# Attention ramp in another order, tokens laid out chunk by chunk, the row of maxima turned by TensorE

## Chip, cores and metric

One core of one Trainium2 chip. The metric is the device time of one execution in microseconds (us), the median of three runs. TensorE (PE) multiplies, its weight loads (PEld) overlap the products; VectorE (DVE), ScalarE (ACT) and GpSimd (POOL) do the rest; SyncE (SP) issues most of the DMAs, GpSimd and ScalarE a few through queues of their own.

## What is computed

An attention over hash buckets, then two feed-forward layers. The change touches the attention alone.

```python
B, H, S, D = 2, 8, 768, 64          # 16 heads of 768 tokens, 64 wide; 6 hash bits
q_bits = q @ proj > 0 ; k_bits = k @ proj > 0
mask = bucket(q_bits)[:, None] == bucket(k_bits)[None, :]
scores = where(mask, q @ k.T / 8, -1e9)
attn = exp(scores - scores.max(-1)) ; attn /= attn.sum(-1) + 1e-9
x = attn @ v                        # then a top-1 mixture of 8 experts and a gated layer
```

## The kernel before, in words

The whole kernel is one stream of instructions per engine, written out by hand: what a Python function emits first stands first in its engine's queue, and an engine that waits holds everything behind it.

The attention stage takes the 16 heads one after the other. A head has 768 keys and 768 queries, cut into `NC` = 6 chunks of `P` = 128 keys; a step `k` is one chunk of one head (96 steps, 6 per head). For each head four tiles stand ready in one of four `sets`: `X` and `K2` hold the scaled high halves of queries and keys and, in rows 64 to 75, the signs of the hash bits; `X` has the row of the queries' maxima in row 76, and `K2` has -1 there, so that one product subtracts the maximum. `K1` and `Y` hold high and low halves crosswise. The steps of a head:

- `prep` (L396) and, for the first three heads, `prep0` (L379): ScalarE makes the high half `hi`, VectorE (GpSimd for heads 0 and 1) the low half `lo`, DMAs of SP bring them to their rows; `put_bits` (L409) brings the signs, two DMAs of SP. `bits` (L419) makes the signs of four heads at a time: TensorE passes (L428), then two passes of VectorE (L417).
- `mx` (L448) takes one chunk of 128 queries against all keys, two products (L454), and VectorE reduces each to its maximum (L457). The chunk's queries are every sixth column, `c::NC`, because query `6p + c` is partition `p` of chunk `c`. After the sixth chunk VectorE makes `top` (L460), 128 x 6, and a DMA (L461) writes it as one row of `X`.
- `scores` (L463): per chunk of keys two halves of 384 queries, two products each (L471, L472), and ScalarE's exponential (L473), which also puts the queries into the order chunk by chunk.
- `high` and `low` (L478, L485) split the exponentials in two halves of 16 bits; `pv` (L489) multiplies them with the values, for two steps at once at odd `k`; `evac` (L521) moves a head's result out.

The values come in groups of four heads (`load_v`, `vmax`, `vscale`, `vsplit`, `vgate`): their largest value fixes a scale (`vscale`, small products L610 and L619 and a chain of small VectorE passes), then `vsplit` (L711) makes their halves, ScalarE the high one (L717), VectorE the low one (L719).

The order: lines 729 to 789 write the ramp up to the first scores, then a loop over `k` (L871) emits per step: what is due before it, ScalarE's high half of step `k-1`, the scores of `k`, the low half of step `k-2` (GpSimd), the maxima of the chunk eight steps ahead (`AHEAD` for the first eight steps, from `Q['ac']`), the value products at odd `k`, what is due after it. `at`, `spread` and `stages` give due times in steps; `load_r` loads a head's queries and keys (384 KB, six buffers). `heat` issues products of zeros that nobody reads. The maxima of head `h` are complete in step `6h - 3`, and its first scores are step `6h`.

## Time and profile before

| | us |
|---|---|
| median of three runs (661.36 to 662.96) | 661.85 |
| the profiled execution | 664.08 |
| its span, first to last instruction | 662.3 |
| first exponential of the attention starts | 19.55 |
| last stage of the attention is over, about | 230 |

TensorE is busy for 95% of the span, VectorE 71%, ScalarE 66%, GpSimd 35%. The chain of work that ended last can be followed back to 230.74 us, where the program branches; the attention stage before it has to be read from tables of stretches and from the engines in order of time. TensorE's products are pipelined: a product's own duration is longer than its distance to the next, so distances between starts are what counts.

### The profile page before, as it was taken

What the parts mean: (1) busy time and instruction counts of PE and PEld (TensorE: products, weight loads), DVE (VectorE), ACT (ScalarE), POOL (GpSimd) and SP (SyncE); (2) the same over time, 40 slices, a digit from 0 to 9 for tenths busy, and PEclk for the clock granted to TensorE, in tenths of its full rate; (3) what the DMA queues carried; (4) which work ended last, traced back from release to release, by engine and by line L of the source; (5) the groups of instructions that cost most, each with busy time, mean ns of one, the idle gap of its engine ahead of it and who ended that gap; (6) DMA issues with size and microseconds to landing.
All of it is one profiled execution on the core that took longest, in us unless ns stands there. A gap on an engine that the chain in (4) does not pass through costs nothing.

```text
span 662.3 us, 14355 instructions
## 1 busy us (share of the span) xinstructions
PE 630.1 (95%) x5497; PEld 469.5 (71%) x5497; DVE 472.1 (71%) x1042; ACT 435.1 (66%) x880; POOL 232.2 (35%) x217
## 2 busy tenths in 40 slices
PE   6999999999999799999999999999999999999892
PEld 2678889889888669999999995555555555555440
DVE  6788988888879888888888888888888342222410
ACT  8658868878878746777776755455545585555820
POOL 6457879879896052111566300000000030000021
PEclk9999999999999989999999999999999999999997
DMA  5645864774465158777677643443441020000011
GB/s 195 175 125 136 243 168 125 237 184 126 103 176 187 57 174 309 242 249 236 214 248 253 212 138 107 141 154 131 127 147 46 0 80 17 0 1 1 0 50 52
DMA packets 37843, 92.18 MB, mean 139 GB/s; under 512 B 8986, under 2 KB 14362, under 8 KB 37762
## 3 DMA queue, kind: packets, MB, share of 16 engines
q1 hardware_dynamic: 34674, 83.75, 41.9%
q0 software_dynamic: 2400, 7.36, 3.2%
q8 instruction: 46, 0.75, 0.5%
q14 instruction: 35, 0.29, 0.1%
q10 hardware_dynamic: 688, 0.03, 0.1%
HBM read 67.14 MB, written 6.29 MB: 111 GB/s over the span
## 4 chain that ended last, share of the span: by engine, by line
PE 55%; ACT 3%; DMA 3%; DVE 2%; issue 1%; POOL 0%; POOLq 0%
PE psg L1332 17%; PE pso L1359 15%; PE psy L1110 11%; PE psh L1083 10%; DMA out_dram<-os,inv 3%; ACT junk L1286 2%; PE psa L1060 1%; ACT gh L1342 1%; DVE rl L1335 1%; DVE wl L164 1%; PE heat L1162 0%; ACT rl L1334 0%; ACT wh L158 0%; ACT hh L1086 0%; PE heatt L335 0%
## 5 line engine op out<-in xcount | busy, mean ns | idle before, releaser
L487 POOL TENSOR_TENSOR plo<-pf,phi 128x768 f16<-128x768 f32 x86 | 144.9, 1706 | 32.8 <-ACT phi L481 16.7
L457 DVE TENSOR_REDUCE mx<-psm 128x1 f32<-128x384 f32 x192 | 96.8, 550 | 20.6 <-PE psm L454 19.9
L473 ACT ACTIVATE pf<-pst 128x384 f32<-128x384 f32 x192 | 83.4, 486 | 40.3 <-PE pst L472 35.8
L1374 POOL DMA_INDIRECT out_dram<-os,inv x12 | 12.1, 1012 | 272.6 <-DVE os L1366 244.3
L164 DVE SCALAR_TENSOR_TENSOR wl<-raw,wh 128x1024 f16<-128x1024 f32 (+1 forms) x68 | 82.5, 1216 | 6.2 <-ACT wh L158 5.4
L1332 PE MATMUL psg<-yTh,ch 128*128 128x512 f16 (+1 forms) x256 | 83.4, 326 | 3.2 <-DVE rl L1335 3.2
L1332 PE MATMUL psg<-yTl,ch 128*128 128x512 f16 (+1 forms) x256 | 83.4, 326 | 0.0
L1332 PE MATMUL psg<-yTh,cl 128*128 128x512 f16 (+1 forms) x256 | 83.4, 326 | 0.0
L1335 DVE SCALAR_TENSOR_TENSOR rl<-rl,psg 128x512 f32<-128x512 f32 x64 | 35.0, 551 | 64.4 <-ACT rl L1334 64.0
L471 PE MATMUL pst<-Y,K 128*128 128x384 f32 x192 | 75.7, 394 | 2.3 <-ACT pf L473 2.3
L1332 PEld LDWEIGHTS <-ch 128*128 128x128 f16 x512 | 50.1, 98 | 35.9
L481 ACT ACTIVATE phi<-pf 128x768 f16<-128x768 f32 x85 | 71.7, 844 | 1.9
L1359 PE MATMUL pso<-ch,gh 128*128 128x512 f16 x192 | 72.8, 379 | 0.0
L1359 PE MATMUL pso<-ch,gl 128*128 128x512 f16 x192 | 72.8, 379 | 0.0
L1359 PE MATMUL pso<-cl,gh 128*128 128x512 f16 x192 | 72.8, 379 | 0.0
L158 ACT ACTIVATE wh<-raw 128x1024 f16<-128x1024 f32 (+1 forms) x68 | 67.4, 998 | 0.8 <-DVE offs L959 0.8
L1359 PEld LDWEIGHTS <-gh 128*128 128x128 f16 x384 | 37.6, 98 | 42.3
L454 PE MATMUL psm<-K,X 76*128 76x384 f32 x192 | 64.3, 419 | 2.8 <-DVE mx L457 1.1
L472 PE MATMUL pst<-X,K 77*128 77x384 f32 x192 | 66.3, 346 | 0.5 <-DMA X<-top 0.5
L1110 PE MATMUL psy<-hh,wl 128*128 128x224 f16 x256 | 66.3, 259 | 0.2 <-DVE wl L164 0.2
L1110 PE MATMUL psy<-hh,wh 128*128 128x224 f16 x256 | 66.3, 259 | 0.0
L1110 PE MATMUL psy<-hl,wh 128*128 128x224 f16 x256 | 66.3, 259 | 0.0
(243 smaller groups left out, 1485.6 us busy)
## 6 DMA issues: line engine op xcount, KB each, us to landing
raw<-in_w_dram SPq DMA_DIRECT2D x64, 512.0 KB
rc<-in_win_dram SPq DMA_DIRECT2D x16, 512.0 KB
rc<-in_wout_dram SPq DMA_DIRECT2D x16, 512.0 KB
r<-in_qk_dram SPq DMA_DIRECT2D x16, 384.0 KB
K<-hi SPq DMA_DIRECT2D x26, 192.0 KB
vr<-in_v_dram SPq DMA_DIRECT2D x4, 768.0 KB
vt<-in_vt_dram SPq DMA_DIRECT2D x8, 384.0 KB
K<-lo SPq DMA_DIRECT2D x16, 192.0 KB
```

Of the source, the lines that this page charges most:

```text
L158: act.activation(wh[e, i][:, c : c + n], r, AF.Copy, scale=(S1, S2)[i // 2])
L164: dve.scalar_tensor_tensor(out=wl[e, i][:, c : c + n], in0=r, scalar=(S1, S2)[i // 2], in1=wh[e, i][:, c : c + n], op0=ALU.mult, op1=ALU.s ...
L457: dve.tensor_reduce(out=mm[:, c, n : n + 1], in_=ps[:, :HS], axis=AX.X, op=ALU.max)
L471: pe.matmul(ps[:, :HS], st["K1"][:, kc], st["Y"][:, qc], start=True, stop=False)
L472: pe.matmul(ps[:, :HS], st["K2"][0:77, kc], st["X"][0:77, qc], start=False, stop=True)
L473: act.activation(pf.rearrange("k (c n p) -> k c n p", c=NC, n=2)[:, :, n], ps[:, :HS].rearrange("k (p c) -> k c p", c=NC), AF.Exp, scale=0 ...
L481: act.activation(phi_t[k], pf_t[k], AF.Copy)
L487: eng.tensor_tensor(out=plo_t[k], in0=pf_t.pop(k), in1=phi_t[k], op=ALU.subtract)
L1083: pe.matmul(ps, l[:, c], r[:, k], start=n == 0, stop=n == 3 * KD - 1)
L1110: pe.matmul(ps, l, r, start=n == 0, stop=n == 3 * KF - 1)
L1332: pe.matmul(ps, l, x, start=n == 0, stop=n == 3 * KD - 1)
L1359: pe.matmul(po[blk][s], l, r, start=first and n == 0, stop=last and n == 2)
```

## The change

- The host lays out queries, keys and values so that the tokens of a chunk (`6p + c` for all `p`) lie together. `mx` then reads a contiguous block of `X`, and the exponential writes straight through.
- The row of maxima: `top` is turned by a transpose on TensorE into 6 x 128, VectorE copies it to a tile `rowm`, and a DMA of six pieces writes the row. `turn` is called in the step after the one that ends the head's maxima, ahead of the next `mx`.
- The ramp: the first head's maxima have a filler product behind each chunk, its row is turned after half of the sign passes, the first scores come ahead of the products of the scale, `put_bits` for heads 1 and 2 uses SP for `X` and GpSimd's queue for `K2`, the rest of `pre[1]`, `pre[2]` and the load of head 4 come later.
- Values of heads 0 and 1: ScalarE also scales `r` in place, GpSimd subtracts for the low half.
- Due times: `pre[2]` ends at 5.5; head 3 is prepared at 7 and 8.25 in place of 2.25 and 5.25; loads of heads 8 to 15 come at -11.5, -10.75, -10 and -4 steps from the group's first step in place of -2 to -1.25; one chunk of maxima moves from step 2 to step 1 and one from step 3 to step 2.

```diff
-'ac': (0, 0, 2, 4, 6, 7, 8, 10)
+'ac': (0, 1, 3, 4, 6, 7, 8, 10)
...
-        top = pa.tile([P, NH, NC], F32R, tag="top", name="top")
+        top = pa.tile([P, NH, NC], F32, tag="top", name="top")
+        rowm = [pa.tile([NC, P], F32R, tag=f"rm{i}", name=f"rm{i}") for i in range(2)]
+        turns = []
...
         def put_bits(h):
             st = sets[h % 4]
+            q = pool if h < 3 else sp
...
-            sp.dma_start(out=f32(st["K2"])[D : D + 12], in_=f32(b)[o + 12 : o + 24])
+            q.dma_start(out=f32(st["K2"])[D : D + 12], in_=f32(b)[o + 12 : o + 24])
...
                 for n in range(2):
                     for i in range(4):
                         dot(n, i)
-                yield
+                    yield
...
-                    ps[:, :HS], st["X"][0:76, c::NC], st["K2"][0:76, n * HS : (n + 1) * HS], start=True, stop=True
+                    ps[:, :HS], st["X"][0:76, c * P : (c + 1) * P], st["K2"][0:76, n * HS : (n + 1) * HS], start=True, stop=True
...
-                sp.dma_start(out=f32(st["X"])[76:77, :].rearrange("o (p c) -> o p c", c=NC), in_=f32(top)[:, h])
+                turns.append(h)
+
+        def turn(h):
+            ps = ps_m.tile([P, 512], F32, tag="m", name=f"pstop{h}")
+            pe.transpose(ps[0:NC, 0:P], top[:, h], ident)
+            dve.tensor_copy(rowm[h % 2], ps[0:NC, 0:P])
+            row = f32(sets[h % 4]["X"])[76:77, :].rearrange("o (c p) -> o c p", c=NC)
+            sp.dma_start(out=row, in_=f32(rowm[h % 2]))
...
-                act.activation(
-                    pf.rearrange("k (c n p) -> k c n p", c=NC, n=2)[:, :, n],
-                    ps[:, :HS].rearrange("k (p c) -> k c p", c=NC), AF.Exp, scale=0.125 / SC / SC,
-                )
+                act.activation(pf[:, qc], ps[:, :HS], AF.Exp, scale=0.125 / SC / SC)
...
             act.activation(t[:, :, o : o + D], r, AF.Copy, scale=s)
+            if h in (0, 1):
+                act.activation(r, r, AF.Copy, scale=s)
             yield
+            lo = t[:, :, VA + o : VA + o + D]
+            if h in (0, 1):
+                pool.tensor_tensor(out=lo, in0=r, in1=t[:, :, o : o + D], op=ALU.subtract)
+            else:
+                dve.scalar_tensor_tensor(
+                    out=lo, in0=r, scalar=s, in1=t[:, :, o : o + D], op0=ALU.mult, op1=ALU.subtract
+                )
...
         for n in range(NC):
             mx(n)
-        run(pre[1])
-        load_r(4)
+            heat(ps_x, "x", 1)
+        next(b0)
+        turn(turns.pop())
         next(b0)
         for i in range(4):
             vmax(0, i)
         vs = vscale(0)
         next(vs)
+        scores(0)
+        next(b0)
+        next(b0)
+        put_bits(1)
         next(vs)
-        next(b0)
-        heat(ps_t, "t", 2)
+        heat(ps_v, "v", 1)
         next(vs)
         next(vs)
-        next(b0)
-        put_bits(1)
-        scores(0)
-        run(b0)
+        put_bits(2)
         run(vs)
-        next(pre[2])
-        put_bits(2)
-        run(pre[2])
+        run(pre[1])
+        load_r(4)
...
+        at(5.5, run, pre[2])
...
-            at(max(0, 24 * (h // 4 - 1) - 2) + h % 4 / 4, load_r, h)
+            at(24 * (h // 4 - 1) + (-11.5, -10.75, -10, -4)[h % 4], load_r, h)
...
-                spread(2.25, prep(h), 3)
+                stages(prep(h), (7, 8.25))
...
+            while turns:
+                turn(turns.pop())
             for n in AHEAD[k] if k < len(AHEAD) else (k + LEAD,):
```

## Rows read from the trace of the kernel before

**Rows 1.** Table of stretches: ends, length, busy us and instructions of each engine.
```profile
core 0: us, PE busy (x) PEld busy (x) DVE busy (x) ACT busy (x) POOL busy (x), PEclk, DMA share, GB/s
128.05:177.65 49.60, 49.31 (x613) 43.69 (x612) 43.14 (x106) 41.44 (x78) 42.03 (x35) 1.00 0.57 148
19.56:52.06 32.50, 30.09 (x268) 22.93 (x268) 25.80 (x58) 21.97 (x41) 18.79 (x11) 1.00 0.44 130
```

**Rows 2.** Groups by line, 70 to 180 us: weight loads, busy us and mean ns.
```profile
L454 PEld LDWEIGHTS psm<-K,X 76*128 76x128 f32 x107 | 29.0, 315 | 0.1
L472 PEld LDWEIGHTS pst<-X,K 77*128 77x128 f32 x106 | 20.2, 190 | 0.0
```

**Rows 3.** TensorE in order of time, two steps: start us, us, instruction.
```profile
107.29 0.42 PE L471 MATMUL pst<-Y,K 128*128 128x384 f32 x1
...
107.91 0.34 PE L472 MATMUL pst<-X,K 77*128 77x384 f32 x1
108.09 0.62 PE L454 MATMUL psm<-K,X 76*128 76x384 f32 x2
108.55 0.27 PE L610 MATMUL psn<-ident,am 128*1 128x128 f32 x1
108.58 0.42 PE L471 MATMUL pst<-Y,K 128*128 128x384 f32 x1
...
111.07 0.42 PE L471 MATMUL pst<-Y,K 128*128 128x384 f32 x1
```

**Rows 4.** ScalarE in order of time, exponentials of the same steps.
```profile
107.99 0.87 ACT L473 ACTIVATE pf<-pst 128x384 f32<-128x384 f32 x2 [0.39 <-PE pst L472]
...
109.65 0.85 ACT L473 ACTIVATE pf<-pst 128x384 f32<-128x384 f32 x2
...
111.77 0.87 ACT L473 ACTIVATE pf<-pst 128x384 f32<-128x384 f32 x2 [0.40 <-PE pst L472]
```

**Rows 5.** Groups by line and shape, ScalarE reading PSUM, whole span.
```profile
L473 ACT ACTIVATE pf<-pst 128x384 f32<-128x384 f32 x192 | 83.4, 486 | 40.3 <-PE pst L472 35.8 <-POOL plo L487 4.3
...
L1086 ACT ACTIVATE hh<-psh 128x224 f16<-128x224 f32 x64 | 22.6, 353 | 17.5 <-PE psh L1083 16.4 <-issue 0.6 <-PE psc L936 0.5
...
L1063 ACT ACTIVATE xh<-psa 128x448 f16<-128x448 f32 x16 | 8.7, 545 | 7.9 <-PE psa L1060 6.7
```

**Rows 6.** In order of time, the row of head 1: SP's issue, TensorE's use.
```profile
33.29 0.51 SPq L461 DMA_DIRECT2D X<-top  x1
...
35.39 0.41 PE L472 MATMUL pst<-X,K 77*128 77x384 f32 x1 [0.46 <-DMA X<-top]
```

**Rows 7.** In order of time, head 4: VectorE ahead of step 22's maxima, TensorE in step 24.
```profile
73.50 0.61 DVE L517 TENSOR_TENSOR xp<-psv,rd 128x432 f32<-128x432 f32 x1
...
76.99 0.34 PE L472 MATMUL pst<-X,K 77*128 77x384 f32 x1
...
110.95 0.27 DVE L613 TENSOR_REDUCE am<-psn 1x1 f32<-1x128 f32 x1
```

**Rows 8.** In order of time, the start: TensorE's groups, VectorE's `top`.
```profile
7.81 5.74 PE L454 MATMUL psm<-K,X 76*128 76x384 f32 x12 [0.77 <-DVE X L417]
13.48 2.79 PE L428 MATMUL psb<-r,pj_sb 128*32 128x384 f32 x16
...
14.22 0.17 DVE L460 TENSOR_REDUCE top<-mx 128x6 fp32r<-128x18 f32 x1
...
18.45 0.69 PE L471 MATMUL pst<-Y,K 128*128 128x384 f32 x1
```

**Rows 9.** In order of time, steps 3 to 6: low halves of values, TensorE behind them.
```profile
26.58 1.62 DVE L719 SCALAR_TENSOR_TENSOR vh<-vr,sc,vh 128x384 f16<-128x384 f32 x1
...
28.73 0.56 PE L454 MATMUL psm<-K,X 76*128 76x384 f32 x1 [0.65 <-DVE mx L457]
...
35.06 2.01 DVE L719 SCALAR_TENSOR_TENSOR vh<-vr,sc,vh 128x384 f16<-128x384 f32 x1
```

**Rows 10.** In order of time, step 9's wait for signs; a low half on VectorE.
```profile
46.85 0.63 PE L563 MATMUL psg<-vt,wg_sb 128*32 128x256 f32 x6 [1.11 <-DVE b L417]
...
53.53 1.18 DVE L372 SCALAR_TENSOR_TENSOR lo<-r,hi 128x768 fp32r<-128x768 f32 x1
```

**Rows 11.** Waits from 77 to 90 us: total us, times, longest.
```profile
PEld psb L428 <- DMA r<-in_qk_dram: 0.9, 1, 0.9
```

**Rows 12.** DMA issues of GpSimd's queue: count, size, median us to landing.
```profile
K<-fill POOLq DMA_DIRECT2D x4, 3.0 KB, 3.2
```

More of the change, by code (lines that the diff above doesn't have):

```diff
@@ L641, in any_unmatched @@
         def any_unmatched():
-            dve.tensor_scalar(out=nm, in0=f32(top), scalar1=-0.5, scalar2=None, op0=ALU.is_le)
+            dve.tensor_scalar(out=nm, in0=top, scalar1=-0.5, scalar2=None, op0=ALU.is_le)
             u = ph.tile([P, NH // 2], F32, tag="un", name="un")
@@ L1522 @@
     q, k, v = inputs["q"], inputs["k"], inputs["v"]
[L1523 to L1525 removed]
+    qk = np.concatenate([q.transpose(0, 1, 3, 2), k.transpose(0, 1, 3, 2)], axis=2).reshape(NH, P, P, NC)
+    qk = qk.transpose(0, 1, 3, 2).reshape(NH, P, S)
+    vv = v.reshape(NH, P, NC, D).transpose(1, 0, 2, 3).reshape(P, NH * NC * D)
+    vt = v.reshape(NH // 2, 2, P, NC, D).transpose(0, 1, 4, 3, 2).reshape(NH // 2, P, S)
     proj = inputs["proj"]
```

9 lines of the change are left out of this document (1 added, 8 removed).

## The prediction

> **What bounds the kernel now.** I read the table of stretches first, because the change touches only the attention stage. Twenty-four chunk steps in the middle of that stage take 49.60 us, 2.07 us each, and TensorE is busy for 49.31 of them, while VectorE, ScalarE and GpSimd stand at 43.1, 41.4 and 42.0; the first twelve steps take 32.50 us, 7.7 more than twelve in the middle, with ScalarE and GpSimd idle for a third or more [rows 1]. So there are two places to gain in: the ramp, where engines wait for each other, and the steady steps, where TensorE is nearly full. A busy share over a pipelined engine does not say what sets the pace, so I went on to TensorE in order of time for two neighbouring steps, one without and one with the value products. The step without takes 107.29 to 108.58, 1.29 us; the one with takes 108.58 to 111.07, 2.49 us [rows 3]. Together 3.78, and ScalarE, read beside it, needs 1.66 for a step when nothing holds it (107.99 to 109.65) and then waits 0.40 for the product of the next [rows 4]. The long step is paced by TensorE alone. The short one is a tie: TensorE has about 1.26 us of work in it, and ScalarE frees the score buffer 0.5 us after its first exponential starts at 107.99, which gives the same 108.5.
>
> Everything after the attention stage (from about 230 us) is untouched, so a shift in it is carried to the end one for one. The profiled execution has a span of 662.3 and took 664.08; the median of the three runs is 661.85, 2.2 below. I make the sum as a difference and apply it to the median.
>
> **Contiguous weights for the products of the maxima.** The only products whose stationary operand is read with a step of six columns are those of L454. Their weight load takes 315 ns on the mean, that of the equally tall operand of L472 takes 190 [rows 2]. On the path this shows as spacing: L471 and L472 follow each other at 0.18 us (107.91 to 108.09), while the pair of L454 takes 0.46, from 108.09 to 108.55, that is 0.23 each [rows 3]. With the new order I take 0.18, so 0.05 less per product and 0.10 per step. In the long step this is on the path, in the short one ScalarE's tie eats it. There are 42 pairs of steps after the first twelve; in the last six no such products are left, so 36 x 0.10 = 3.6 us. Bounds: nothing, if VectorE (43.1 of 49.6 busy) takes over as the pace; 7.2, if both steps gain.
>
> **Exponentials without the shuffle.** Each reads and writes 384 elements in a permuted order now and takes 486 ns. Contiguous reads of 224 and 448 elements take 353 and 545, which puts 384 at 490 [rows 5]. I cost this at nothing.
>
> **The row of maxima by TensorE.** Now the 128x6 maxima go straight to one row by a DMA. New are, per head, a transpose (TensorE), a copy (VectorE) and the DMA, all issued one step later. The nearest row for the transpose is L610: it takes 0.27, but the next product starts 0.03 after it [rows 3], so it costs 0.03 to 0.27, in the short step; I take 0.05, hidden in ScalarE's tie, and 14 x 0.27 = 3.8 if that cover is gone. The transpose waits for VectorE's last maximum; queued behind it on TensorE are the two next products of the maxima. The copy waits for the transpose; behind it on VectorE are the next two reductions. On SP the DMA waits for the copy, with loads and stores behind it.
>
> The dearer point is when the row lands. From issue to use a row takes 2.1 us (33.29 to 35.39), and that wait of 0.46 was the only one it caused before [rows 6]. In the steady steps the new chain starts when VectorE has moved out the previous head: 74.11 for the head shown, then the copy (0.27, as the nearest row of one partition by 128), the issue, and 2.1: 76.5. The product that needs it starts at 76.99 [rows 7]. So about half a microsecond is left; the same reading for heads 2 to 15 leaves between none and 1.4, with four heads at or about none, and the shorter steps take another 0.1. I take 1.5 us in all for heads that wait. Bounds: none, and 9 (14 x 0.65, a landing of 3 us at every head).
>
> **Loads of heads 8 to 15 earlier.** Eight loads move forward by up to ten steps, past the issues of two heads' preparation in SP's queue; their buffers are free by then (the last readers of heads 2 to 5 run before), so SP does not stand. What goes is one wait, 0.9 us for r before the sign products of the third group [rows 11]; it occurs once, the last group does not have it. Gain 0.9. Bounds: 0 to 0.9.
>
> **The ramp, in order.** Start: twelve products of the maxima take 5.74, sixteen sign passes 2.79, and the first scores start at 18.45 although the maxima were ready at 14.39 [rows 8]. Now the row is turned after half of the passes: 13.5 + 1.4 + 0.27 + 0.27 + 2.1 = 17.6 for its landing, about 1 us before the second score product of now. Against this stand six fillers between the products, and a second chunk that now comes behind the two products of the scale, which wait for VectorE (four maxima of the values, the signs). Bounds -1.4 (half of the passes) to +0.8; I take -0.2. Bits by two queues: GpSimd issues two DMAs that wait for the signs; behind them stands its first low half, which has nothing to do before the first exponential.
>
> Steps 2 to 5: VectorE's low half of head 0's values takes 1.62 there, and TensorE stands 0.65 behind it at 28.73; head 1's takes 2.01 [rows 9]. Both go to GpSimd, which is busy for 18.8 of the ramp's 32.5 [rows 1], for one more ScalarE pass each. Head 3's first half (one ScalarE pass, four DMAs) leaves these steps too. I take -1.5; bounds -3 to 0, the latter if GpSimd's cover is gone and 1.6 comes back through it.
>
> Step 6: the row of head 1 now comes a step later, where it already was the last to come [rows 6]: copy, transpose and a step's place less what VectorE is ahead, +0.4 (0 to 1.0). Steps 7 to 9: head 3's preparation comes here, with VectorE's pass of 1.18 in the place where VectorE already holds TensorE for 1.11 at 46.85 [rows 10]: +1.0 (0 to 1.2). Its six DMAs have two steps to land before head 3's first maxima; the wait just named covers that.
>
> Ramp: -0.2 - 1.5 + 0.4 + 1.0 = -0.3. **Sum:** -3.6 + 0 + 1.5 - 0.9 - 0.3 = -3.3 us, span 659.0, and the median 661.85 - 3.3 = 658.5.
>
> **Rivals.** *The row becomes the bound.* If a landing takes 3 us beside other transfers rather than 2.1, each of 14 heads waits about 0.5 to 0.6 more: 14 x 0.55 = 7.7 more than in my sum, 666. It decides from the point where less than 0.5 us is left, which is where [rows 7] stands; against it, six pieces of 512 bytes replace 128 of 24. Price 666, slower. *Another engine takes the pace.* VectorE gets a copy per head and has only 13% idle; if it or ScalarE gives back the 3.6, the time is 662, the same as before. *More is gained.* If both steps gain (7.2 instead of 3.6), no head waits and the ramp gives its 3: -7.2 - 0.9 - 3 = 11 less, 651. *The bits come late.* From issue to landing, four small DMAs of GpSimd's queue took 3.2 us [rows 12] against the 2.1 of SP's row; the first product of head 1's maxima now stands one step earlier in TensorE's order, ahead of scores, so twice 1.1 us would be lost: 660.7. The Trainium skill has a rule that speaks for this one (SBUF — State Buffer, section "SBUF: two separate sides", the note on VectorE blocking a DMA): a DMA from GpSimd's queue can starve while VectorE holds the port that both share. No row here shows such a starving; by the rule the 3.2 would grow by what VectorE runs at that time.
>
> **How the numbers follow.** Forecast, 656 to 660.3: 0.42. Row as bound: 0.15. Another engine: 0.16. Late bits: 0.09. More gained: 0.18. A measurement of this kernel tells 0.3%, 2 us, from no change. Below 659.9 lie the case of more gained and nearly all of the forecast's, with some of the others: 0.62. Between 659.9 and 663.8 lie most of the late bits and of the other engine: 0.22. Above: 0.16. The range 652 to 665 leaves out the outer halves of the two extreme cases; the forecast's own is 656 to 660.3.
>
> **What would show it.** The pair of L454 at 0.36 in place of 0.46, and pairs of steps at 3.68 in place of 3.78, would show the first step right; pairs at 3.78 with ScalarE's 0.40 gone or VectorE full would show it wrong. Waits of the second score product for the row, at the first chunk of each head, show the second: I expect them at four to six heads, a few tenths each. The step in which the third group's signs are made should lose its wait for r. In the ramp the sixth exponential should start about 1.5 us sooner, and that lead should be nearly gone by the tenth. The prediction is wrong if the row waits at most heads by over half a microsecond, or if the weight load of L454 stays near 315.

## The result, and the profile after

The changed kernel takes 669.93 us, the median of four runs (667.63 to 671.0); before took 661.61 beside it (659.99 to 662.96). The ratio is 1.0114, interval 1.0083 to 1.0145: 1.1% slower, where 658.5, half a percent faster, was predicted. The profiled execution took 671.0, its span is 669.3 against 662.3.

The first thing to read is what the change set out to do in the steady steps. Groups by line of after, 70 to 180 us (busy us, mean ns; then the idle time ahead of them), against [rows 2, 5]:

```profile
L457 PEld LDWEIGHTS psm<-K,X 76*128 76x128 f32 x105 | 19.2, 195 | 2.2 <-DVE mx L460 1.3
L482 PEld LDWEIGHTS pst<-X,K 77*128 77x128 f32 x104 | 20.3, 195 | 1.9 <-DMA X<-rm 1.9
...
L483 ACT ACTIVATE pf<-pst 128x384 f32<-128x384 f32 x104 | 45.1, 486 | 19.6 <-PE pst L482 16.5 <-POOL plo L494 2.3 <-POOL vh L738 0.4
```

The weight load of the products of the maxima fell from 315 ns to 195, what the other operand of that height takes. The exponential has 486 ns as before. TensorE in order of time, a short step and a long one (start, us, instruction), against [rows 3]:

```profile
150.23 0.44 PE L481 MATMUL pst<-Y,K 128*128 128x384 f32 x1
...
151.03 0.51 PE L457 MATMUL psm<-K,X 76*128 76x384 f32 x2
151.49 0.45 PE L481 MATMUL pst<-Y,K 128*128 128x384 f32 x1
...
152.33 0.51 PE L457 MATMUL psm<-K,X 76*128 76x384 f32 x2
152.68 0.21 PE L506 MATMUL psv<-vh,phi 128*128 128x73 f16 x1
```

In the long step the pair takes 0.35 (152.33 to 152.68; the median of such pairs from 70 to 180 us is 0.354, in before 0.457), in the short one still 0.46, because the next product waits for ScalarE. So the saving is there, 0.10 per pair of steps, as worked out. The loss has to be elsewhere, and the table of stretches shows where. I cut the attention, finer than in [rows 1], at the starts of the exponentials of steps 0, 12, 84 and 95. After:

```profile
core 0: us, PE busy (x) PEld busy (x) DVE busy (x) ACT busy (x) POOL busy (x), PEclk, DMA share, GB/s
19.62:55.77 36.15, 29.37 (x272) 21.31 (x271) 27.62 (x68) 23.16 (x42) 22.67 (x16) 0.95 0.54 142
55.77:206.60 150.83, 146.21 (x1837) 121.54 (x1836) 134.28 (x327) 123.96 (x230) 124.19 (x97) 0.98 0.62 168
206.60:229.80 23.20, 20.11 (x244) 16.09 (x243) 21.77 (x52) 17.97 (x34) 9.22 (x9) 0.93 0.38 125
```

Before, the same cuts (columns as above):

```profile
19.55:52.05 32.50, 30.09 (x268) 22.93 (x268) 25.81 (x58) 21.96 (x40) 18.79 (x11) 1.00 0.45 130
52.05:203.14 151.09, 148.34 (x1825) 131.25 (x1824) 129.93 (x315) 124.02 (x232) 126.33 (x98) 1.00 0.64 171
203.14:222.84 19.70, 18.20 (x244) 15.32 (x243) 18.11 (x50) 17.66 (x34) 8.06 (x8) 1.00 0.39 132
```

The first exponential starts at 19.62 against 19.55. Then: first twelve steps +3.65, the next 72 -0.26 (where 3.6 should have been won), the last eleven +3.50, and the rest of the program as long as before; together the 7.0 us of the two spans. TensorE is busy for less of each stretch, and its granted clock, 1.00 in all three before, is 0.95, 0.98 and 0.93. So single long waits are to be sought. Taking the distance of one step's first exponential to the next in both traces leaves, beside step 1 (+1.7, which step 3 gives back), three places where steps are over a microsecond longer: steps 9 and 11 (+2.3, +1.2), 41 and 43 (+1.8, +2.6), 87 (+3.3).

**Step 9.** SP's issues (start, us):

```profile
38.19 0.42 SPq L596 DMA_DIRECT2D vr<-in_v_dram  x1
39.73 0.47 SPq L402 DMA_DIRECT2D X<-hi  x1
```

VectorE (idle time and its releaser in brackets):

```profile
42.45 0.95 DVE L374 SCALAR_TENSOR_TENSOR lo<-r,hi 128x768 fp32r<-128x768 f32 x1
...
46.18 0.55 DVE L600 TENSOR_REDUCE am<-vr 128x1 f32<-128x384 f32 x1 [0.64 <-DMA vr<-in_v_dram]
46.65 1.57 DVE L732 SCALAR_TENSOR_TENSOR vh<-vr,sc,vh 128x384 f16<-128x384 f32 x1
...
48.61 0.60 DVE L420 TENSOR_SCALAR b<-psb,pj_sb 128x384 fp32r<-128x384 f32 x1
```

The same pass of VectorE in before:

```profile
45.14 0.66 DVE L719 SCALAR_TENSOR_TENSOR vh<-vr,sc,vh 128x384 f16<-128x384 f32 x1
```

GpSimd in after:

```profile
44.57 5.15 POOL L494 TENSOR_TENSOR plo<-pf,phi 128x768 f16<-128x768 f32 x3 [4.58 <-DVE phi L490]
```

TensorE:

```profile
49.27 0.63 PE L570 MATMUL psg<-vt,wg_sb 128*32 128x256 f32 x6 [3.56 <-DVE b L420]
```

Head 3's transfers now follow the 768 KB load of the next values by 1.5 us. VectorE waits for those values, its next pass takes 1.57 instead of 0.66, the signs behind it come late, and TensorE stands for 3.56 where it stood for 1.11 [rows 10].

So two things lengthen the step: 0.64 us for the values, and 0.9 in a pass that runs beside GpSimd's low halves. The runs below let them be told apart. In the seven profiles with head 3 prepared as in after, VectorE waits 0.5 to 2.7 us for the values, and wait and pass together take 2.15 to 2.22 us (five profiles) or 3.80 and 3.81 (`gap`, `loads_early`). In ten of the other twelve there is no such wait, and the pass takes 0.61 to 0.70. The levels lie some 1.6 us apart, close to the length of one of GpSimd's passes here (5.15 for three). That suggests that it counts less how late the values are than behind which of GpSimd's passes VectorE gets in. And the other two profiles, `contig` and `layout_alone`, have the long pass with the preparation of before. In contig VectorE waits for no values, and still:

```profile
43.59 2.05 DVE L716 SCALAR_TENSOR_TENSOR vh<-vr,sc,vh 128x384 f16<-128x384 f32 x1
```

TensorE there (total us, times, longest):

```profile
PE psg L560 <- DVE b L417: 2.8, 1, 2.8
```

Step 9 takes 7.54 in that execution, with half clock behind it. The late preparation is the way into this stall in after, but not the only one.

**Step 41.** SP's issues:

```profile
111.27 0.58 SPq L362 DMA_DIRECT2D r<-in_qk_dram  x1
111.95 0.39 SPq L559 DMA_DIRECT2D vt<-in_vt_dram  x1
112.38 0.92 SPq L362 DMA_DIRECT2D r<-in_qk_dram  x2
113.96 0.75 SPq L471 DMA_DIRECT2D X<-rm  x1
```

TensorE, the product that needs the row of head 7:

```profile
118.54 0.44 PE L482 MATMUL pst<-X,K 77*128 77x384 f32 x1 [1.62 <-DMA X<-rm]
```

Three of the loads that the change moved, 384 KB each, and a fourth transfer go out right in front of the row; from issue to use it takes 4.6 us, where the row of head 1 took 2.1 in before [rows 6].

**Step 87.** VectorE of after:

```profile
208.36 1.02 DVE L460 TENSOR_REDUCE mx<-psm 128x1 f32<-128x384 f32 x2 [0.15 <-PE psm L457]
209.30 3.36 DVE L251 TENSOR_TENSOR ge<-pos,edges 128x30 f32<-128x30 f32 x1
```

GpSimd at that time:

```profile
204.25 8.11 POOL L494 TENSOR_TENSOR plo<-pf,phi 128x768 f16<-128x768 f32 x5
```

TensorE, behind VectorE:

```profile
214.05 0.44 PE L457 MATMUL psm<-K,X 76*128 76x384 f32 x1 [2.06 <-DVE mx L460]
```

The same pass of VectorE in before:

```profile
205.89 0.18 DVE L251 TENSOR_TENSOR ge<-pos,edges 128x30 f32<-128x30 f32 x1
```

GpSimd in before:

```profile
199.49 6.50 POOL L487 TENSOR_TENSOR plo<-pf,phi 128x768 f16<-128x768 f32 x4
206.73 1.74 POOL L487 TENSOR_TENSOR plo<-pf,phi 128x768 f16<-128x768 f32 x1 [0.74 <-ACT phi L481]
```

A pass over 30 elements takes 3.36 us, until 0.3 after the end of GpSimd's run at 212.36; in before it took 0.18 and fell on the end of GpSimd's run, where GpSimd pauses. VectorE's reductions out of PSUM (208.36) keep their half microsecond each in the midst of that run.

Behind each of the three waits the trace's record of the granted clock goes to half, 1.2 GHz: 50.9 to 54.3, 119.1 to 125.9 and 214.7 to 218.1. Before has no such stretch between 21.9 and 230.1.

### The profile page after: what moved, and what is told of

It reads as the page before. It is cut to its first block, busy times and chain, and to the rows that moved or that the text cites. A ratio compares the mean times of both kernels' runs of the same rounds, so it can differ in the third digit from the quotient of the medians.

```text
span 669.3 us, 14415 instructions
## 1 busy us (share of the span) xinstructions
PE 627.8 (94%) x5516; PEld 457.6 (68%) x5516; DVE 481.5 (72%) x1056; ACT 436.4 (65%) x882; POOL 235.9 (35%) x221
## 4 chain that ended last, share of the span: by engine, by line
PE 54%; DMA 3%; ACT 3%; issue 3%; DVE 2%; POOL 0%; POOLq 0%; DVEq 0%
PE psg L1347 16%; PE pso L1374 15%; PE psy L1125 11%; PE psh L1098 10%; DMA out_dram<-os,inv 3%; ACT junk L1301 1%; PE psa L1075 1%; ACT gh L1357 1%; DVE rl L1350 1%; DMA xg<-xd,ids 1%; DVE wl L164 0%; ACT rl L1349 0%; POOL xg L1056 0%; DVE hl L1102 0%; POOL out_dram L1389 0%
## 5 line engine op out<-in xcount | busy, mean ns | idle before, releaser
L1347 PEld LDWEIGHTS <-ch 128*128 128x128 f16 x512 | 50.1, 98 | 35.9
L506 PE MATMUL psv<-vh,phi 128*128 128x73 f16 x576 | 65.8, 200 | 0.0
```

The source lines that it names most:

```text
L1347: pe.matmul(ps, l, x, start=n == 0, stop=n == 3 * KD - 1)
```

## The experiments

In the list, "step n takes" is the distance from the first exponential of step n to that of the next. Each run was measured beside before again; its ratio is to that. The seven edits of after up to `gap`, and `mended`, leave 4.8 to 8.5 us of the loss, and the interval of each overlaps that of after, so the medians alone show no single gain; what an edit did is read from its trace.

**layout_alone**: before with the new order of tokens and the turned row, nothing else of the change.

```diff
-st["X"][0:76, c::NC]
+st["X"][0:76, c * P : (c + 1) * P]
...
+        def turn(h):
...
-        next(b0)
+        next(b0)
+        turn(turns.pop())
```

> The kernel before with the chunk-by-chunk layout and the turned row alone; ramp, due times and loads as before (the first head's row is turned behind its sign passes). Theory (the layout gains 0.1 us per pair of steps and the loss sits at three places that other parts of the change made: step 9, step 41 with the loads, step 87): the pair of products of the maxima at 0.36 us, step pairs at 3.68, no wait of 1 us or more for the row after head 1, first exponential and head 1's row 0.5 us later each, total 2 to 4 us under the kernel before. Rival (the turned row itself costs, at many heads): waits for the row at most heads, and a total of the kernel before or more.

Measured: 670.43, ratio 1.0128 (1.009 to 1.0165). Neither ramp nor loads are needed for the loss. The profile is of its longest execution, 678.2. The first exponential starts at 22.5, 3 us late. Waits from 14 to 26 us:

```profile
PE psn L616 <- DVE am L610: 2.6, 1, 2.6
DVE rm L468 <- PE pstop L467: 1.9, 1, 1.9
```

VectorE's copy of the first row waits 1.9 us for the transpose, which TensorE does behind the sixteen sign passes. Behind the copy stand VectorE's maxima of the values (they start at 16.68 instead of 14.31), and TensorE waits 2.6 for them at the products of the scale (0.52 in before). The row itself goes out at 18.24, behind head 1's low half and a load in SP's queue, but the score product waits only 0.5 for it. Step 50 takes 4.03 instead of 1.72, waiting for r: four loads due four steps earlier stood behind the row, which waited for VectorE's copy. Step 83 takes 4.9, and step 9 6.71. My theory was that this kernel would gain; it fell.

**loads_old**: after with the due times of the loads of before.

```diff
-            at(24 * (h // 4 - 1) + (-11.5, -10.75, -10, -4)[h % 4], load_r, h)
+            at(max(0, 24 * (h // 4 - 1) - 2) + h % 4 / 4, load_r, h)
```

> The changed kernel with the loads of heads 8 to 15 at their due times of before. Theory (head 7's row lay behind three loads in the DMA queue, and TensorE's half clock that followed cost more than the wait): the wait at step 42 (1.6 to 1.9 us) and the slow step 43 (2.6 us more) vanish, the wait for r at the third group's signs (1.0 to 1.3) returns: 3 us less than the changed kernel. Rival (the row is late at head 7 for another reason, such as VectorE's place in the order): the wait of step 42 stays, the total is 1 us above the changed kernel.

Measured: 669.6, ratio 1.0142 (1.0095 to 1.019). Steps 41 and 43 are back at 2.05 and 2.81, so the stall there is the loads'. But the wait for r of [rows 11] is back at step 26 (2.86) and new at step 50 (3.96): early loads cost about as much at head 7 as they save at the signs. I had expected 3 us; the median is 0.3 below that of after.

**prep_old**: after with heads 2 and 3 prepared as in before.

```diff
+        run(pre[2])
...
-        at(5.5, run, pre[2])
...
-                stages(prep(h), (7, 8.25))
+                spread(2.25, prep(h), 3)
```

> The changed kernel with heads 2 and 3 prepared where they were before (head 2 ahead of the loop, head 3 at 2.25 and 5.25). Theory (head 3's low half on VectorE at step 8.25 and its DMAs ahead of the values of the next group stretch step 9 from 5.1 to 7.5 us and so send TensorE to half clock until step 11): step 9 back at about 5.1, no half clock at 50 us, steps 2 to 5 longer by 0 to 2 us: 1.5 to 3.5 us less than the changed kernel. Rival (step 9 is long for GpSimd's phase or the values' load alone): step 9 stays above 6.5, the total within 1 us of the changed kernel.

Measured: 669.21, ratio 1.0108 (1.0072 to 1.0144). Step 9 takes 5.13, as in before, and step 11 2.21; steps 41, 43 and 87 keep 3.8, 4.2 and 5.4. In its profiled execution step 7 took 4.86, with half clock from 38.0 to 44.8. The step came out as expected, the total did not (0.7 less in the medians, of 1.5 to 3.5).

**both_old**: the two edits together.

```diff
+        run(pre[2])
...
+            at(max(0, 24 * (h // 4 - 1) - 2) + h % 4 / 4, load_r, h)
...
+                spread(2.25, prep(h), 3)
```

> The changed kernel with both of these undone. Theory: the two losses are apart and add up: 4.5 to 6.5 us less than the changed kernel, so 2 to 4 us above or at the kernel before, with what is left of the loss at step 87 (3.3 us) where VectorE's small operation waits for a gap in GpSimd's work. Rival (one stall's time comes back elsewhere): 3 us less or under.

Measured: 667.16, ratio 1.0118 (1.0053 to 1.0182); three of its four runs lie between 662.4 and 668.5. The profiled one, the fastest, has no half clock between 7.7 and 652.8, and its step 12 starts where that of before does. Step 50 takes 3.73, step 87 3.95. The rival was right: the two gains do not add up to 4.5 to 6.5.

**clock_held**: after with products of zeros ahead of two of the three waits.

```diff
+        def hold(n, tag):
...
+        at(9.3, hold, 14, "v")
+        at(41.4, hold, 7, "m")
```

> After, with products of zeros that nobody reads put ahead of two long waits of TensorE: fourteen ahead of step 9's wait for VectorE's signs (3.6 us in after) and seven ahead of the wait for the row of head 7 in step 42 (1.6 us in after). The waits themselves are untouched. If each wait costs twice, once as a wait and once more because the granted clock falls to half behind it (50.9 to 54.3 and 119.1 to 125.9 in after), then both stretches of half clock are gone, step 11 takes 2.3 instead of 3.5 and step 43 takes 2.8 instead of 5.4, while steps 9 and 41 keep 7.5 and 3.9: 3.8 us in all, a median of about 666. If the clock follows something else than TensorE standing idle, the two steps keep their 3.5 and 5.4 and the median stays at 670 or goes up by what the products of zeros take.

Measured: 666.9, ratio 1.0075 (1.0049 to 1.0101). The two stretches in clock_held (columns as in the tables above; the granted clock is the number ahead of the DMA share):

```profile
48.00:58.00 10.00, 9.16 (x99) 6.83 (x98) 7.05 (x18) 6.52 (x12) 5.50 (x4) 1.00 0.55 123
118.00:128.00 10.00, 10.00 (x116) 8.15 (x115) 7.75 (x21) 8.07 (x16) 7.39 (x5) 1.00 0.91 261
```

The same stretches in after:

```profile
48.00:58.00 10.00, 8.73 (x83) 7.34 (x84) 7.01 (x17) 6.32 (x12) 5.36 (x4) 0.83 0.44 101
118.00:128.00 10.00, 9.46 (x67) 7.68 (x68) 4.81 (x12) 5.26 (x10) 5.84 (x4) 0.66 0.87 236
```

The long steps stay (9 and 41 take 6.96 and 3.49), and the clock stays up. Step 11 takes 2.54 instead of 3.51, step 43 2.69 instead of 5.42: 3.7 us in the two steps behind the waits, from work that nobody reads. Such a wait of TensorE costs twice here. What is left of it in all differs: steps 40 to 43 together take 9.8 instead of 13.1, but steps 8 to 11 14.6 instead of 14.7, because in this execution TensorE also waited in step 8 (0.7 for r, in a weight load) and in step 10 (0.84 for head 3's bits). The medians are 3.0 apart, with intervals that overlap.

**row_direct**: after without the turn.

```diff
-                turns.append(h)
+                sp.dma_start(out=f32(st["X"])[76:77, :].rearrange("o (p c) -> o p c", c=NC), in_=f32(top)[:, h])
...
-            while turns:
-                turn(turns.pop())
```

> After without the turn: no transpose, no copy by VectorE; the 128x6 maxima go straight to the row by one DMA, issued where the sixth chunk's maxima are made, one step earlier than in after. The row is then in the order of before and not in that of the chunks, so the maximum subtracted from a query's scores is that of another query, which cancels in the division; all else is as in after. If the late row is what costs, the waits for the row in the steady steps (6.1 us on TensorE and its weight loads in seven of them) go, steps 41 and 43 fall from 3.9 and 5.4 to about 2.1 and 2.8, and the median is 664 to 666. If the waits come from the loads in front of the row in SP's queue and not from the turn, step 41 keeps over 3 us and the median stays within 1.5 us of 670.

Measured: 667.02, ratio 1.007 (1.0044 to 1.0096). The sum came near my 664 to 666, the place did not. SP's issues:

```profile
111.23 1.43 SPq L360 DMA_DIRECT2D r<-in_qk_dram  x2
112.77 0.51 SPq L462 DMA_DIRECT2D X<-top  x1
```

Waits from 110 to 128 us (total us, times, longest):

```profile
PE pst L473 <- DMA X<-top: 3.4, 1, 3.4
```

The row still follows the three loads and is waited for longer (3.4 us in place of 1.6; steps 41 and 43 take 5.84 and 4.78). So at head 7 the loads make the row late, not the turn. Step 87 is short here, 1.95, but step 83 takes 3.27 instead of 2.01. Against after, the turn costs 2.9 us by the medians.

**loads_early**: after with those loads ahead of the preparation.

```diff
-            at(24 * (h // 4 - 1) + (-11.5, -10.75, -10, -4)[h % 4], load_r, h)
+            at(24 * (h // 4 - 1) + (-13.5, -13.4, -12.3, -4)[h % 4], load_r, h)
```

> After with the loads of heads 8 to 10 and 12 to 14 moved forward once more, by 2 to 2.65 steps, so that they are issued ahead of the preparation of heads 4 and 8 in SP's queue and not between that and the row. If the late row of head 7 comes from the three loads in front of it, the wait of step 42 is gone, steps 41 and 43 fall from 3.9 and 5.4 to about 2.1 and 2.8, and no wait for r comes back at the signs of the third group: about 4 us less, a median of 666. If the transfers only move and the row waits elsewhere, or the loads now delay the preparation of heads 4 and 8, the steps between 10 and 45 lose as much and the median stays at 670.

Measured: 667.63, ratio 1.0095 (1.0058 to 1.0131). Steps 41 and 43 take 2.18 and 2.70, step 26 takes 1.67, and no wait for r or for the row is left between 84 and 122 us. This settles step 41. The rest was not better: step 9 took 9.9 in this execution, with 2.7 us of waiting for the values.

**gap**: after with step 83's low half by VectorE.

```diff
-            return k < STEPS - END or k - STEPS + END in Q["ll"]
+            return k < STEPS - END - 1 or k - STEPS + END in Q["ll"]
```

> After with one low half of the exponentials, that of step 83, made by VectorE instead of GpSimd, so that GpSimd has a pause before the low half of step 85. In after, GpSimd makes five of them without a pause (204.25 to 212.33) and a VectorE pass over 30 elements that reads two operands from SBUF takes 3.36 us, ending when GpSimd ends; TensorE then waits 2.1 us. If such passes of VectorE stand still while GpSimd runs without a pause, that pass takes under 1.7 us here, step 87 falls from 5.4 to between 2.1 and 3.5, and no half clock follows it: 2 to 4 us less, for about 1 us more work of VectorE. If the 3.36 us has another reason (the engine's queue, a late semaphore), step 87 stays at 5 us or more.

Measured: 667.71, ratio 1.0092 (1.0058 to 1.0125). The pass over 30 elements takes 1.07, step 87 3.72 (a little over what I gave it), and no half clock follows. Step 9 takes 9.9 in this profile too.

**contig**: before with the new order alone, the row straight.

```diff
-st["X"][0:76, c::NC]
+st["X"][0:76, c * P : (c + 1) * P]
...
-                act.activation(
-                    pf.rearrange("k (c n p) -> k c n p", c=NC, n=2)[:, :, n],
-                    ps[:, :HS].rearrange("k (p c) -> k c p", c=NC), AF.Exp, scale=0.125 / SC / SC,
-                )
+                act.activation(pf[:, qc], ps[:, :HS], AF.Exp, scale=0.125 / SC / SC)
```

> Before, with the new order of tokens alone: contiguous blocks of queries for the products of the maxima and exponentials written straight through; the row of maxima goes out by the DMA of before (so the maximum subtracted from a query's scores is another query's, which cancels in the division); ramp, due times and the rest as in before. Against the run with layout and turn (670.4) it takes the turn away. If the contiguous weights give 0.10 per pair of steps and the turn is what costs, pairs of steps in the middle take 3.68 and the median is 656 to 659.5. If the new order brings the losses itself, by running ahead into waits and half clock that before does not meet, the pairs still take 3.68, but the median stays at 661.5 or over.

Measured: 658.67 beside 662.25 of before, ratio 0.9944 (0.9927 to 0.9962): 3.6 us, the first term of my sum. That the digit agrees is luck, since the interval reaches from 2.5 to 4.8. In its trace, the weight load, 70 to 180 us:

```profile
L454 PEld LDWEIGHTS psm<-K,X 76*128 76x128 f32 x108 | 19.8, 190 | 1.3 <-DVE mx L457 1.2
```

The lead over before grows by 0.10 per pair, from 0.02 at step 48 to 1.46 at step 76, and steps 12 to 83 together take 147.45 instead of 151.09. Against layout_alone the median is 11.8 us less: that much the turn cost in that place.

**contig_early**: the same with the early loads.

```diff
-            at(max(0, 24 * (h // 4 - 1) - 2) + h % 4 / 4, load_r, h)
+            at(24 * (h // 4 - 1) + (-13.5, -13.4, -12.3, -4)[h % 4], load_r, h)
```

> The same with the loads of heads 8 to 15 earlier (13.5, 13.4, 12.3 and 4 steps before the group's first step). If the wait for r at the signs of the third group is worth what the other runs show (1.3 us) and the transfers meet nothing else, 1 to 1.5 us less than the new order alone. If the row of a head waits behind these loads in SP's queue, step 41 takes over 3 us and the median is the same or higher.

Measured: 657.73, ratio 0.9925 (0.9907 to 0.9943). It has the lowest median here, 0.9 below contig, with intervals that overlap, so the gain of 1 to 1.5 from the loads is not shown.

**contig_again**: the same program, for a second profile.

> The new order with early loads and the straight row (median 657.7, profiled at 662.4 with half clock from 11.2 to 24.9) once more. If its faster executions are those without half clock in the ramp, a profile near 657 shows none between 12 and 25, a first exponential near 17.4, and steps 1 and 2 at 2.0 and 2.6 instead of 3.7 and 2.9; the steady steps are the same to 0.1.

Measured: 659.15, ratio 0.9976 (0.9945 to 1.0006), single runs from 657.4 to 664.4; this interval includes no difference from before. The profiled execution took 662.17, so the question that I put to a profile near 657 was not answered. It has no half clock between 22.1 and 206.4, but step 87 took 5.73, with half clock from 206.4 to 213.3 behind the wait. VectorE there:

```profile
202.23 1.71 DVE L251 TENSOR_TENSOR ge<-pos,edges 128x30 f32<-128x30 f32 x1
203.86 2.46 DVE L484 TENSOR_TENSOR plo<-pf,phi 128x768 f16<-128x768 f32 x1
```

GpSimd there:

```profile
197.38 8.11 POOL L484 TENSOR_TENSOR plo<-pf,phi 128x768 f16<-128x768 f32 x5
```

In the first profile of this very program VectorE had:

```profile
204.78 0.30 DVE L251 TENSOR_TENSOR ge<-pos,edges 128x30 f32<-128x30 f32 x1
205.00 0.95 DVE L484 TENSOR_TENSOR plo<-pf,phi 128x768 f16<-128x768 f32 x1
```

GpSimd's run was one of four, with a pause behind it:

```profile
198.55 6.48 POOL L484 TENSOR_TENSOR plo<-pf,phi 128x768 f16<-128x768 f32 x4
205.67 1.80 POOL L484 TENSOR_TENSOR plo<-pf,phi 128x768 f16<-128x768 f32 x1 [0.65 <-PE pst L472]
```

So the clash of step 87 is no part of the turn as such; in these two profiles it comes with a GpSimd run of five passes and stays away with one of four and a pause.

**ramp_alone**: before with the ramp of after, and nothing else; as an edit of after:

```diff
-        top = pa.tile([P, NH, NC], F32, tag="top", name="top")
+        top = pa.tile([P, NH, NC], F32R, tag="top", name="top")
...
-        turn(turns.pop())
...
-st["X"][0:76, c * P : (c + 1) * P]
+st["X"][0:76, c::NC]
...
-            at(24 * (h // 4 - 1) + (-11.5, -10.75, -10, -4)[h % 4], load_r, h)
+            at(max(0, 24 * (h // 4 - 1) - 2) + h % 4 / 4, load_r, h)
```

> After with the order of tokens, the exponentials' shuffle, the straight row of maxima and the due times of the loads all as in before: what is left of the change is the ramp. If the ramp costs what the leads of after show (step 9 at 7.5 us in place of 5.1, because the 768 KB of values and head 3's six transfers are under way together, and half clock behind it), the tenth step starts 2 us or more later than in before and the median is 664 to 667. If the ramp is worth nothing either way, as the prediction summed it up (-0.3), the median is within 1 us of before.

Measured: 665.03, ratio 1.0042 (1.0028 to 1.0056): 2.8 us slower, as in the first of my two cases. The first exponential starts 1.6 us sooner, and that lead holds up to step 9 (1.85 there). Step 9 then takes 8.25 and step 11 3.68 (5.13 and 2.27 in before), and at step 12 it is 2.95 behind.

**mended**: after with prep_old, loads_early and gap together; the turned row stays.

```diff
+        run(pre[2])
...
+            return k < STEPS - END - 1 or k - STEPS + END in Q["ll"]
...
+            at(24 * (h // 4 - 1) + (-13.5, -13.4, -12.3, -4)[h % 4], load_r, h)
...
+                spread(2.25, prep(h), 3)
```

> After with three edits: heads 2 and 3 prepared at the times of before, the loads of heads 8 to 15 at 13.5, 13.4, 12.3 and 4 steps ahead, the low half of step 83 by VectorE. The turned row of maxima stays. If the losses of after are the three waits that these edits take away and the clock behind them, step 9 takes 5.1, steps 41 and 43 2.1 and 2.8, step 87 under 4, and the median is 657 to 661. If the turn costs at every head, or the granted clock falls behind other waits, it stays at 664 or over.

Measured: 667.08, ratio 1.0078 (1.0048 to 1.0108); I had 657 to 661. Each single wait did what was asked: step 9 takes 5.02, 41 and 43 take 2.41 and 2.70, 87 takes 3.72. The first twelve steps still take 35.9, with step 2 at 4.5 and half clock from 29.2 to 32.6, and the last eleven 22.1. Mending the three places I had read was not enough.

**turn_act**: layout_alone with the row issued by ScalarE's queue.

```diff
-            sp.dma_start(out=row, in_=f32(rowm[h % 2]))
+            act.dma_start(out=row, in_=f32(rowm[h % 2]))
```

> Before with the new order of tokens and the turned row (the run of 670.4), the row's DMA issued by ScalarE's queue instead of SP's. The turned row costs 11.8 us there against the straight one (658.7). If the reason is SP's queue, in which the row waits for VectorE's copy and the loads wait behind the row, and the first row waits behind head 1's low half and the load of head 4, then the waits for r go (steps 26 and 50 from 3.3 and 4.0 to 2.7 and 1.7), the first exponential starts 2 us sooner or more, and the median is 662 to 666. If the reason lies in the transpose, its PSUM buffer and VectorE's copy, or if ScalarE now stands behind the copy, the median stays over 668.

Measured: 682.76, ratio 1.0332 (1.0302 to 1.0363), the slowest of all. Steps 26 and 50 lose their wait for r (2.32 and 1.66), so SP's queue was the reason there. The first exponential starts at 22.06, only 0.5 sooner than in layout_alone, where I had expected 2 or more: the queue was not what made it late. And ScalarE now stands. Its groups from 60 to 230 us, of turn_act:

```profile
L487 ACT ACTIVATE phi<-pf 128x768 f16<-128x768 f32 x66 | 55.6, 842 | 6.5 <-DVE mx L459 4.7 <-ACT pf L482 0.6
...
L723 ACT ACTIVATE vh<-vr,sc 128x384 f16<-128x384 f32 x13 | 8.1, 623 | 5.3 <-DVE mx L459 3.2 <-DVE un L650 2.0
```

In layout_alone the idle times of these two groups are 1.6 and 0.0. In the same stretch TensorE waits for the row six times, 7.6 us in all. In both queues, SP's and ScalarE's, the row's DMA waited for VectorE's copy and held what stood behind it.

**turn_early**: contig_early with the turn of layout_alone; the first head's row is turned after half of the sign passes and ahead of head 1's low half.

```diff
-        run(pre[1])
-        load_r(4)
         next(b0)
+        turn(turns.pop())
+        run(pre[1])
+        load_r(4)
+        next(b0)
...
+            while turns:
+                turn(turns.pop())
```

> The new order of tokens with the early loads (657.7 with the straight row), and the row turned: for the first head after half of the sign passes and ahead of head 1's low half in SP's queue, for the others a step later as in after; the row goes by SP. No load is due at the steps in which SP waits for a row. If queues were the cost of the turn, step 50 takes 1.7, the first exponential starts within 0.7 us of before, and the median is 659 to 662. If the turn costs by itself, as the step 87 of after suggests (GpSimd's run without a pause comes back with it), it is 664 or over.

Measured: 665.48, ratio 1.0068 (1.0045 to 1.0091); steps 26 and 50 take 1.66 to 1.67, and still the turn costs 7.8 us against contig_early. The first exponential starts at 20.42, 0.9 after that of before. The waits for the row from 18 to 236 us in turn_early (total us, times, longest):

```profile
PE pst L481 <- DMA X<-rm: 2.4, 4, 1.0
```

The same in contig_early:

```profile
PE pst L472 <- DMA X<-top: 2.6, 4, 0.8
```

The sums are the same. But these two executions, 663.9 and 662.4, are not 7.8 us apart, and the places differ: at step 89 the turned row is waited for, in all three profiles of this program and its two variants below (0.95 to 1.4 us), the straight row in none. And here, too, the copy of the first row waits for the transpose (0.9), and TensorE 1.2 for the maxima of the values behind it.

**turn_gap**: turn_early with step 83's low half by VectorE.

```diff
+            return k < STEPS - END - 1 or k - STEPS + END in Q["ll"]
```

> The same with the low half of step 83 made by VectorE. If the clash of VectorE with GpSimd's run is what is left of the turn's cost, step 87 or 83 loses its 1.5 to 3.3 us and the median is 1 to 3 us under that of the run before it. If VectorE's extra microsecond costs as much, there is no difference over 1 us.

Measured: 664.55, ratio 1.0042 (1.0019 to 1.0064), 0.9 under turn_early with intervals that overlap, so no gain is shown. Steps 83 and 87 take 3.33 and 2.01 in its profile, 3.04 and 1.95 in that of turn_early: the clash of step 87 was not there to be taken away.

**turn_again**: turn_early once more, for a second profile.

> The run before last (new order, early loads, row turned early; median 665.5, profiled at 663.9) once more, for a second profile. If the turned row costs by TensorE's clock falling behind its short waits, a profile over 665 shows more or longer stretches of half clock in the attention than 10.5 to 24.1, and the length of its steps outside of those stretches is that of the first profile. If it costs by waits alone, the clock pattern is the same and single steps are longer.

Measured: 665.84, ratio 1.0064 (1.0043 to 1.0084), single runs from 660.9 to 667.0, and the profiled one is the 660.9. Both profiles of the turned row are thus of its shortest executions and both of the straight row of its longer ones; they show steps 5, 41 and 89 longer by 0.4 to 0.8 in either pair, but not the 7 us of the medians. My question asked for a profile over 665 and got none.

Two things on record go further. The first is the granted clock of each single run, on the mean and as a share of full speed. Of the runs at 0.989 or more, the six with the turned row (turn_early, turn_again) took 660.9 to 667.0, 664.9 on the mean, the seven with the straight row (contig_early, contig_again) 656.1 to 660.2, 658.3 on the mean. With the clock alike the turn still costs 6.7 us, so half clock is not what makes it. The second is a comparison by stretches, three profiles with the turned row (turn_early, turn_again, turn_gap) against three with the straight row (contig, contig_early, contig_again), the shortest of each: 1.2 us more up to the first exponential (20.01 against 18.78), 1.2 in the first twelve steps (33.33 against 32.17), 1.8 in steps 12 to 83 (149.28 against 147.45) and 0.8 in the last eleven (20.15 against 19.34). That is 5.0 us, an estimate, since each shortest stretch may come from another execution. The start goes with the order on VectorE, and the end with the row at step 89; what makes the rest, and where it lies in a typical execution, stays open.

## Why the prediction was wrong, point by point

The gain was forecast rightly, the losses were not: the steps that failed are the price of the turned row (+1.5), steps 7 to 9 of the ramp (+1.0), "SP does not stand" for the loads, and that no term counted what follows a wait of TensorE.

- **Contiguous weights, -3.6.** Right in mechanism, place and size: 0.46 to 0.35 per pair, long step only, and 3.6 us in contig.
- **Exponentials without the shuffle, 0.** Right: 486 ns before and after.
- **Loads earlier, -0.9.** The gain is there in after's trace (steps 26 and 27 are 1.3 shorter), though contig, with the loads as in before, has step 26 at 1.73 too. The step that failed is "SP does not stand": I asked whether SP would wait for buffers, not what would follow the loads in its queue. Head 7's row does, and waited 1.6 on TensorE; with the clock behind it 4.4 us went there, more than the gain (shown by loads_old and loads_early).
- **Row of maxima, +1.5.** Waits of the second score product for the turned row are 3.5 us in four places in after, so the count was as forecast; the longest, 1.6, is head 7's, which is the loads'. The failed step is that the price of the row is when it lands. The prediction names the other price, that the copy waits for the transpose and holds what stands behind it on VectorE, and puts nothing for it. At the first head VectorE waited 0.9 (turn_early) to 1.9 us (layout_alone) for the transpose, and TensorE then 1.2 to 2.6 for what the copy had held back. By the medians the turn costs 2.9 us in after (row_direct), 6.7 to 7.8 on contig_early and 11.8 on contig. Of the 11.8 the trace of layout_alone shows 3 us at the start and SP's queue behind the row (1.6 and 2.4 at steps 26 and 50, against contig); of the 6.7 to 7.8 some 5 are located by stretch, and 2 of these have a cause (the start and step 89); the rest is not explained. The slack that the prediction read from [rows 7], none to 1.4 us per head, was not where most of it was lost.
- **Ramp, -0.3.** Mis-sized: +2.8 (ramp_alone). Its profile starts 1.6 us sooner rather than 0.2, and steps 2 to 5 added nothing to it. A start read from one profile says little, though: loads_old, prep_old and both_old, with the instructions of after up to there, start at 17.4 to 17.5, with full clock from 7.3 to 7.7 us on, and after at 19.6, with full clock from 16.7 on. The dear term is steps 7 to 9, which I took at +1.0 with a bound of 1.2: it cost 3.1, and 1.4 more in step 11. I had counted VectorE's pass and given head 3's six DMAs two steps to land, but not seen that they are under way together with 768 KB of values for which VectorE waits, and that VectorE's pass, once late, stretches beside GpSimd's low halves (1.34 there instead of 0.66).
- **Bits by GpSimd's queue.** Waits for them were there, 1.3 us for `K2` and 0.8 for `X` in step 1, as the rival put it, but step 3 gave them back (1.65 instead of 3.49). From issue to landing that queue had 3.2 us in [rows 12] and 2.9 in after. No run shows VectorE starving such a DMA: its issue waited for VectorE's results.
- **What no term had.** First the clock. A wait of 1.6 to 3.6 us of TensorE was followed by 3.4 to 6.8 us at 1.2 GHz, and with the clock held up the two steps behind such waits were 3.7 us shorter (clock_held). The Trainium skill (TensorE: Matmul & The Clock Gate, section "HAM oscillation — how this bites in real kernels") describes such a stall as one after which the products start slow again; the trace agrees. Second, VectorE behind GpSimd: 3.36 us for what takes 0.18. The Trainium skill (SBUF — State Buffer, section "SBUF: two separate sides") says that a VectorE operation with two operands in SBUF and a GpSimd operation exclude each other for a whole instruction. The direction agrees. In clock_held the pass came in at a border of GpSimd's passes (1.53 us), in after it stood beyond such a border, until the run was over.

The range failed for the same reason as the sum. Each cost was bounded as a wait that ends; none had the second bill behind it. The rival "the row becomes the bound" came nearest with 666, by waits at every head that no profile shows.

Put on before, the parts nearly add up: new order -3.6, ramp +2.8 and turn +7.8 make 668.6 from 661.6, close to the 669.9. Taken out of after they do not: row_direct, loads_old, prep_old and both_old, which each take a real stall away, win 0.3 to 2.9 with intervals that overlap. Each of the four profiles has a long step elsewhere (step 83 at 3.27 in row_direct, step 50 at 3.96 in loads_old and 3.73 in both_old, step 7 at 4.86 in prep_old). Step 50 is the loads' own; that the other two came because a stall was removed, and not with that one execution, is not shown.

## What to carry to other kernels

A contiguous stationary operand was worth what the rows of before promised, so the small local gain could be read off; what has to be costed is everything that the rest of the change puts next to something else. For each DMA that is moved, list what stands behind it in its queue and what large transfer is under way with it. For each new operation that waits for another engine, list what it holds back on its own. Where TensorE is the pace, a new wait of some microseconds should be priced with the slower clock that follows it, and products of zeros in the wait can be the cheaper choice; here they won 3.2 us around one wait and 0.1 around another.

The lowest medians are those of contig_early (657.7 and 659.2 in its two measurements, beside 662.3 and 661.4 of before; the interval of the second includes no difference). It subtracts another query's maximum, which cancels in the division as long as the exponentials stay in range, so it is no drop-in replacement.

## What the runs showed of the hardware

- TensorE at half clock (1.2 GHz) in after: behind the wait of step 9 (3.56 us) from 50.9 to 54.3; behind that of step 41 (1.62 on the products) from 119.1 to 125.9; none with products of zeros in the same places (clock_held).
- VectorE passes with two operands in SBUF stretch while GpSimd makes low halves without a pause: 0.18 to 3.36 (30 elements), 0.95 to 2.46 (768), 0.61 to 2.05 (384 elements, step 9 of contig). Reductions out of PSUM beside them do not (0.51 each in step 87 of after). In step 9, VectorE's wait and pass together lie at levels some 1.6 us apart (0.61 to 0.70, 2.05 to 2.22, 3.80), a GpSimd pass taking 1.7.
- Executions of one program differ more once it has such stalls: 663.3 to 672.2 for clock_held against 660.6 to 664.8 for before in the same measurement. One profile is one draw of these.
